# Weight loads moved from SyncE's queue to GpSimd's, unread steps left out and a new order, in an RWKV7 and SwiGLU kernel

## The chip, the cores and the metric

The kernel runs on one core of one Trainium2 chip. The metric is the device time of one execution in microseconds (us). A core has TensorE (PE; its weight loads are shown apart as PEld), VectorE (DVE), ScalarE (ACT), GpSimd (POOL) and SyncE (SP), which only issues DMAs here. POOL and ACT issue DMAs too, each in its own in-order stream.

## What is computed

The reference, cut to what matters. The shapes are B = 4, H = 8, S = 768 and D = 40; the feed-forward part has 3072 tokens, width 320 and inner width 1536.

```python
state = zeros((B, H, D, D))
for t in range(S):
    y[:, :, t] = einsum('bhd,bhde->bhe', rt, state)
    Sa = einsum('bhde,bhe->bhd', state, at)
    state = state * wt[:, :, None, :] - einsum('bhd,bhe->bhde', Sa, bt)
    state = state + einsum('bhd,bhe->bhde', vt, kt)
x = y.transpose(0, 2, 1, 3).reshape(B * S, H * D)
rms = sqrt(mean(x * x, axis=-1, keepdims=True) + 1e-06)
xn = x / rms * rms_g
g = xn @ w_gate
out = (g / (1 + exp(-g)) * (xn @ w_val)) @ w_out
```

The last state is returned to nobody: only y goes on. The feed-forward weights come in as 8-byte floats, and the kernel turns them into 4-byte floats itself.

## The kernel before

The sequence is cut into 24 chunks of 32 steps. Each chunk goes through three stages, which the code names front, inverse and main.

**front(c)** loads w, a, k, b and v of the chunk (tiles wan, kbn, wn, VU; from SP and ACT's queues for chunk 0, from POOL's for all later ones), turns them by transposes on PE, and forms by a ladder of levels 1, 2, 4, 8, 16 the products of decays. At each level it updates K (on the page `K<-K,T`; the copied half on ACT), the left factors A (at level 16 the tile aP, called Aend16 below) and the decay products T (T[32] at the end, called T32). The level's products give LT, a triangular matrix for each head and batch. LT goes out to a DRAM scratch sB and comes back, laid out otherwise, as M (8 DMAs on SP). At the end K, decayed over the whole chunk, is transposed into KN[32].

**inverse(c)** solves the triangular system on DVE in the tile Yi: 15 pairs of tensor_tensor for the first five chunks, 31 steps for later ones. The result goes out to the scratch sY and comes back into LT (8 more DMAs on SP).

**main(c)** multiplies with the state (aP times ST), solves with LT, updates the state (KN[32] times VU, the piece called update, plus the decayed old state Sdec, which uses T[32]), forms the scores and the levels, and makes y. It then takes the root mean square (a sum of squares ss, to the power -0.5 on POOL, called pow below), turns the rows and scales them by the norm's weights gcol into xg.

**feed(g)** is the feed-forward part for one or two chunks together: gate and value products on PE, SiLU on ACT, the product hT on DVE, the output product po on PE, and the result to DRAM by SP.

**narrow** turns the raw weights into 4-byte floats. The 1536 inner columns are 12 slices of 128; a slice has two halves, and 2f + h is called unit 0 to 23 in this document. An even unit has two raw loads, an odd one four, 72 in all. The raw data is laid into a tile that is not yet in use: unit u uses one of four, so it waits until unit u - 4 has been converted. Then come seven operations, with two integer tensor_scalar and three scalar_tensor_tensor operations of 480 elements among DVE's, and two on ACT.

None of these pieces is issued in the order of the code. Each call of `plan.add` makes a piece; a list ORDER names for each step which of the pieces comes next (a count from the first one not yet issued), and PAIRS says which of three PSUM pairs each room gets. So the instruction order of every engine is written out: an engine takes its pieces in this order, and a piece that waits holds back all that follow it on its engine or queue. The before kernel has 6003 pieces. Line 486 is the helper of DVE's operations, 509, 513 and 516 those of ACT's, 519 POOL's tensor_tensor, 522 and 525 its copies and memsets, 529 the helper of every DMA, 532 matmuls and 535 transposes. The raw loads are at lines 1026 to 1029, the norm's loads at 596, the ladder's end at 779 to 811 and the update at 881 to 888.

Of the kernel before, what the change touches and what calls it, by code (L numbers as in the profile page):

```python
# [16 lines left out]
P = 128  # L17
# [388 lines left out]
def kernel(  # L406
# [187 lines left out]
    for p0, kt, src in ((0, 0, 0), (0, 1, P), (0, 2, 2 * P), (64, 2, 2 * P)):  # L594
        m = min(P, DM - src)
        dma(gcol[p0:p0 + m, kt:kt + 1], moe_rms_g[src:src + m].rearrange("(d o) -> d o", o=1), "g")
# [105 lines left out]
    def kn(z, l, i, n, o):  # L702
        return z["KN"][l][half(i), kn_at(l, n, o)]
# [396 lines left out]
```

## Time and profile before

| What | Value |
|---|---|
| median of three runs | 1037.38 us (1035.87 to 1040.97) |
| the profiled execution: its time, its span | 1039.87 us, 1038.0 us |
| busy PE, DVE, ACT, POOL | 934.5, 790.2, 498.4, 306.6 us |
| share of PE in the chain that ended last | 70% |
| SyncE's queue (q1, with 42.37 MB), POOL's (q0, 22.64 MB) | 18.4%, 11.8% of 16 engines |
| one raw load on SP: 256, 224, 96, 64 KB | 4.4 to 5.5, 3.5, 3.9, 4.1 to 4.2 us to landing (medians) |
| one load on POOL: 40 KB, 80 KB | 2.6 to 2.9, 2.8 to 3.2 us to landing (medians) |

The span runs from the first to the last instruction. Busy time counts an engine's work and not its issue of DMAs, but for POOL, whose DMA instructions are work of its own and are counted. The page cuts the span into 40 slices of 26 us and gives the busy tenths of each; the granted clock of PE is shown beside them, in tenths of full speed. It is

```
PEclk 9957667899999999999999999999999999999999
```

so PE has its full clock only at the very start and from about 187 us on. In SP's view an instruction is the issue of a DMA, shown as SPq with its time; data lands later.

### The profile page before, as it was taken

The page shows a single profiled execution, that of the slowest core. Times are in us where ns is not written, and L with a number is a line of the kernel's source. Part 1 is how long each engine was busy: PE and PEld are TensorE (multiplying, and loading weights), DVE is VectorE, ACT ScalarE, POOL GpSimd, SP SyncE. Part 2 cuts the span into 40 slices and gives each one's busy share as a digit, 9 for nine tenths or more (in the row PEclk, how much of TensorE's full clock was granted, in tenths as well). Part 3 has the DMA queues.
Part 4 walks back from the last instruction along what each step waited for, and adds up shares of the span by engine and source line. Part 5 has one row for each costly group of instructions (what it writes and reads, how often), then busy time and mean ns, then how long its engine had stood idle before and what let it go on. Part 6 is the DMA issues. An engine that isn't in the chain of part 4 may idle for free.

```text
span 1038.0 us, 55525 instructions
## 1 busy us (share of the span) xinstructions
PE 934.5 (90%) x24592; PEld 760.3 (73%) x24592; DVE 790.2 (76%) x2747; ACT 498.4 (48%) x1113; POOL 306.6 (30%) x530
## 2 busy tenths in 40 slices
PE   2546767999999999999999999999999999999998
PEld 2445756877777878777778777777787787788777
DVE  8989978867869778868778679678697787777531
ACT  5566556453454464464454544534534635436131
POOL 9523234221432242233331324123232413400000
PEclk9957667899999999999999999999999999999999
DMA  7675443222242242232231232232322422420100
GB/s 159 145 173 120 99 93 82 56 63 54 43 84 38 47 95 43 60 79 42 59 84 28 62 75 55 55 68 36 76 45 55 81 41 65 75 44 8 43 7 21
DMA packets 147056, 68.89 MB, mean 66 GB/s; under 512 B 121088, under 2 KB 136384, under 8 KB 146816
## 3 DMA queue, kind: packets, MB, share of 16 engines
q1 hardware_dynamic: 128448, 42.37, 18.4%
q0 software_dynamic: 16192, 22.64, 11.8%
q8 instruction: 193, 3.16, 1.3%
q10 hardware_dynamic: 2176, 0.33, 0.2%
q14 instruction: 47, 0.39, 0.1%
HBM read 55.05 MB, written 10.22 MB: 63 GB/s over the span
## 4 chain that ended last, share of the span: by engine, by line
PE 70%; DVE 9%; DMA 7%; SPq 4%; issue 4%; ACT 2%; DVEq 0%; ACTq 0%
PE ps L532 50%; PE po L532 14%; PE ps L535 6%; SPq L529 4%; DVE Yi L486 2%; DMA LT<-sY 2%; DMA sY<-Yi 2%; DVE tmp L486 1%; DMA sB<-LT 1%; DVE LT L486 1%; DVE wf L486 1%; DMA M<-sB 1%; DVE K L486 1%; DVE y L486 1%; DVE As L486 0%
## 5 line engine op out<-in xcount | busy, mean ns | idle before, releaser
L532 PE MATMUL ps<-xg,wf 128*128 128x256 f32 (+3 forms) x1872 | 361.1, 375 | 1.1 <-DVE hT L486 0.9
L532 PEld LDWEIGHTS ps<-xg,wf 128*128 128x128 f32 (+1 forms) x1872 | 267.7, 190 | 49.1 <-issue 13.2
L532 PE MATMUL po<-wf,hT 128*128 128x320 f32 x576 | 179.7, 446 | 1.1 <-issue 1.1
L486 DVE TENSOR_TENSOR hT<-ps,sg 128x256 f32<-128x256 f32 (+1 forms) x156 | 59.8, 398 | 94.1 <-PE ps L532 56.0
L532 PEld LDWEIGHTS po<-wf,hT 128*128 128x128 f32 x576 | 102.9, 189 | 38.6 <-issue 4.0
L486 DVE TENSOR_TENSOR tmp<-Yi,M 128x24 f32<-128x24 f32 (+21 forms) x512 | 106.6, 208 | 17.4 <-DMA M<-sB 4.5
L486 DVE TENSOR_TENSOR Yi<-Yi,tmp 128x24 f32<-128x24 f32 (+21 forms) x512 | 106.8, 209 | 10.6
L509 ACT ACTIVATE sg<-ps 128x256 f32<-128x256 f32 (+1 forms) x156 | 54.0, 369 | 109.8 <-PE ps L532 106.8
L529 POOL DMA_DIRECT2D VU<-in_v_dram x92 | 53.9, 587 | 155.4 <-PE ps L532 134.4
L486 DVE TENSOR_TENSOR K<-K,T 128x512 f32<-128x512 f32 (+1 forms) x192 | 93.2, 501 | 4.4 <-PE ps L532 1.9
L519 POOL TENSOR_TENSOR ss<-ss,mhalf 128x1 f32<-128x1 f32 x24 | 14.3, 596 | 255.1 <-DVE ss L486 255.0
L532 PE MATMUL ps<-Ab,K 64*60 64x56 f32 (+2 forms) x4608 | 76.3, 220 | 12.7 <-issue 2.4
L532 PEld LDWEIGHTS ps<-Ab,K 64*60 64x60 f32 (+2 forms) x4608 | 69.3, 132 | 22.4 <-issue 10.1
L513 ACT COPY KN<-ps 128x640 f32<-128x640 f32 x96 | 65.8, 692 | 38.8 <-DVE LT L486 24.4
L529 POOL DMA_DIRECT2D kbn<-in_k_dram x92 | 54.1, 589 | 98.5 <-PE ps L532 98.5
L486 DVE TENSOR_TENSOR As<-ps,msi 128x256 f32<-128x256 f32 (+1 forms) x168 | 70.9, 453 | 15.5 <-PE ps L532 10.9
L529 POOL DMA_DIRECT2D kbn<-in_b_dram x92 | 54.1, 589 | 82.9 <-PE ps L532 81.3
L532 PEld LDWEIGHTS ps<-As,KN 128*40 128x40 f32 x3072 | 67.3, 128 | 11.6 <-issue 4.1
L532 PE MATMUL ps<-As,KN 128*40 128x32 f32 x3072 | 72.6, 208 | 2.4 <-DVE As L486 1.2
L513 ACT COPY K<-K 128x512 f32<-128x512 f32 x96 | 61.0, 636 | 27.1 <-PE ps L532 11.8
L486 DVE SCALAR_TENSOR_TENSOR Yi<-M,Yi 128x31 f32<-128x31 f32 (+6 forms) x228 | 44.5, 243 | 36.7 <-DMA M<-sB 20.0
L529 POOL DMA_DIRECT2D wn<-in_w_dram x92 | 51.8, 565 | 43.7 <-DVE KN L486 43.5
(131 smaller groups left out, 1503.4 us busy)
## 6 DMA issues: line engine op xcount, KB each, us to landing
M<-sB SPq DMA_DIRECT2D x96, 128.0 KB, 3.0
wan<-in_r_dram SPq DMA_DIRECT2D x24, 160.0 KB, 4.0
kbn<-in_k_dram POOLq DMA_DIRECT2D x92, 40.0 KB, 2.6
kbn<-in_b_dram POOLq DMA_DIRECT2D x92, 40.0 KB, 2.9
VU<-in_v_dram POOLq DMA_DIRECT2D x92, 40.0 KB, 2.7
wan<-in_w_dram POOLq DMA_DIRECT2D x46, 80.0 KB, 3.2
wan<-in_a_dram POOLq DMA_DIRECT2D x46, 80.0 KB, 2.8
wn<-in_w_dram POOLq DMA_DIRECT2D x92, 40.0 KB, 2.8
```

The source lines that it names most:

```text
L486: plan.add("DVE", time + more + each * size(o), 0.087, lambda at: [fn(at(o), *m(at))], [o], aps(*args))
L509: scalar(o, [a], lambda at: nc.scalar.activation(at(o), at(a), f, **kw), aps(acc), 0.1 if f in (AF.Square, AF.Relu) else 0.0)
L513: scalar(o, [a], lambda at: nc.scalar.copy(at(o), at(a)), extra=more)
L519: plan.add("POOL", 0.5, 0.06, lambda at: nc.gpsimd.tensor_tensor(o, a, b, op), [o], [a, b])
L529: plan.add(by, 0.6 if by == "POOL" else 0.45, 0.0, lambda at: queue.dma_start(out=o, in_=i), [o], [i], load=load, since=since)
L532: return o, lhsT, rhs, lambda at: nc.tensor.matmul(at(o), lhsT, rhs, start=start, stop=stop, skip_group_check=True), 4
L535: return o, i, ident, lambda at: nc.tensor.transpose(at(o), i, ident), 2
```

## The change

There are four parts. The raw loads of units 4 to 23 (slices 2 to 11, 60 DMAs) and the four loads of the norm's weights are issued by POOL in place of SP. Steps whose result nobody reads are left out: for chunk 0 the left factors and decays for a state that does not exist yet (aP and T[32]), for chunk 23 the last K and its copy, T[32], KN[32], Sdec and the update of the state. PAIRS is shorter by the two rooms. ORDER is a new list of 5993 pieces. The computed output is the same.

```diff
-        dma(gcol[p0:p0 + m, kt:kt + 1], moe_rms_g[src:src + m]..., "g")
+        dma(gcol[p0:p0 + m, kt:kt + 1], moe_rms_g[src:src + m]..., "g", "POOL")
...
-            K1 = K_.next()
+            if G > 1 or c + 1 < NCH:
+                K1 = K_.next()
...
+            if l == 16 and c == 0:
+                K = K1
+                break
...
-            tt(Tl[2 * l], t[:, :, :, 0], t[:, :, :, 1], MUL)
+            if G > 1 or c + 1 < NCH:
+                tt(Tl[2 * l], t[:, :, :, 0], t[:, :, :, 1], MUL)
...
-        z["KN"][32] = KN_[32].next()
+        if c + 1 < NCH:
+            z["KN"][32] = KN_[32].next()
...
-        if c > 0:
+        if 0 < c < NCH - 1:
             tt(Sdec, ST.rearrange("p n i d -> p (n i) d")[:, :, 0:D], z["T"][32].to_broadcast((P, NI, D)), MUL)
...
-        up = plan.room()
-        pe("update", [mm(up[part(o), i, col(slot(n))], kn(z, 32, i, n, o), VU[half(i), n, o, 0:D]) for n, i, o in each])
+        if c + 1 < NCH:
+            up = plan.room()
+            pe("update", [mm(up[part(o), i, col(slot(n))], kn(z, 32, i, n, o), VU[half(i), n, o, 0:D]) for n, i, o in each])
...
-                else src.bitcast(I32).rearrange("p (f w) -> p f w", w=2), load, since=S0 + S1 * f)
+                else src.bitcast(I32).rearrange("p (f w) -> p f w", w=2), load, "SP" if f < 2 else "POOL", since=S0 + S1 * f)
```

Decoded, the two lists differ as follows around the loads. SP's list before has weights between the DMAs of the first inverses (inverse 1: three sY, four raw loads, a sY, a norm load, an LT, a norm load, three LT); after, the sB, M, sY and LT groups of the first four chunks stand whole, but for the chunk's own r loads and the first M group inside inverse 0's sY. POOL's list after has the 60 raw loads among the loads of the next chunks, the memsets of the start and the pow steps: the first at place 46 of POOL's pieces, unit 13's last three right behind the first VU load of front 2, unit 21's last three behind chunk 1's pow, unit 22's second behind a kbn load of front 5, and unit 23's last three behind chunk 2's pow. DVE's and PE's lists keep the order of the stages; on DVE unit 23 is converted ahead of the first feed's third hT, where before its last three operations came after eight of them.

More of the change, by code (lines that the diff above doesn't have):

```diff
@@ L33 @@
 ORDER = """
[202 rows of a table removed]
[200 rows of a table added]
 """
 PAIRS = """
-01201210121021200021102212200010110200100201020112101002120121012212012212110202010010102012120120012002120020000011
-21210200101022100112022211110111102001222121111021211202221200012011120122122211112120211212100022010102200020101002
-20021101010001010211121111020000111210200010012212120021012112221201202122010201200001101212210212102121021020112110
-12111102101020202122221201022110100022221210101022022002020221211202011101001210222111101200200021222021210111211010
-122221012001120211200102020212021
+01201210010210202012021221120102002012011102100012202011220021012221220001021002101020200111220010221101211112220020
+10110002021210102121022002120211100120101010210201211112201202020220212020012221020202110101022011121211111212011002
+00210201011001020121010110202022122122102201111101020011112000120120122212221011010001212020021112120122220210212211
+12211212002100202200101012210010100111221210000211021201121112111222000202002010212111102110100021211012120220000221
+2102101222020212210001010212012
 """
@@ L595 @@
         m = min(P, DM - src)
-        dma(gcol[p0:p0 + m, kt:kt + 1], moe_rms_g[src:src + m].rearrange("(d o) -> d o", o=1), "g")
+        dma(gcol[p0:p0 + m, kt:kt + 1], moe_rms_g[src:src + m].rearrange("(d o) -> d o", o=1), "g", "POOL")
     blank(eye, 0.0)
@@ L778, in front @@
             t = Tl[l].rearrange("p n (g x) -> p n g x", x=2)
-            K1 = K_.next()
-            if G == 1:
-                tt(K1[:, :, :, 0:16], K[:, :, :, 0:16], t[:, :, None, :, 1].to_broadcast((P, NI, 2, 16)), MUL)
-            else:
-                for x in range(2):
-                    tt(side(K1[:, :, x], l, 0), side(K[:, :, x], l, 0), t[:, :, :, 1, None].to_broadcast((P, NI, G, l)), MUL)
-            kn_ = lambda k: k.rearrange("p n x (g h l) -> p (n x) g h l", h=2, l=l)[:, :, :, 1]
-            copy(kn_(K1), kn_(K))
+            if G > 1 or c + 1 < NCH:
+                K1 = K_.next()
+                if G == 1:
+                    tt(K1[:, :, :, 0:16], K[:, :, :, 0:16], t[:, :, None, :, 1].to_broadcast((P, NI, 2, 16)), MUL)
+                else:
+                    for x in range(2):
+                        tt(side(K1[:, :, x], l, 0), side(K[:, :, x], l, 0), t[:, :, :, 1, None].to_broadcast((P, NI, G, l)), MUL)
+                kn_ = lambda k: k.rearrange("p n x (g h l) -> p (n x) g h l", h=2, l=l)[:, :, :, 1]
+                copy(kn_(K1), kn_(K))
+            if l == 16 and c == 0:
+                K = K1
+                break
             if l == 16:
@@ L807, in front @@
             dma(M[m * BH:(m + 1) * BH].rearrange("p b x -> p (b x)")[:, 0:C * C], sB, "M")
-        z["KN"][32] = KN_[32].next()
-        copy(z["KN"][32].rearrange("p (n o e) -> p n o e", n=N, o=2),
-             turned(K.rearrange("p (n i) x s -> p n (i x s)", i=2), ins=TOP, outs=P)[:, :, :, 0:D])
+        if c + 1 < NCH:
+            z["KN"][32] = KN_[32].next()
+            copy(z["KN"][32].rearrange("p (n o e) -> p n o e", n=N, o=2),
+                 turned(K.rearrange("p (n i) x s -> p n (i x s)", i=2), ins=TOP, outs=P)[:, :, :, 0:D])
         z["aP"] = A
@@ L880, in main @@
                              U[other(i, 4 * q), :, 0:4 * D].rearrange("p o (n d) -> p o n d", n=4), more=0.09)
-        up = plan.room()
-        pe("update", [mm(up[part(o), i, col(slot(n))], kn(z, 32, i, n, o), VU[half(i), n, o, 0:D]) for n, i, o in each])
-        if c == 0:
-            copy(ST_.next()[:, :, :, 0:D].rearrange("p n i d -> p i n d"), up[:, :, 0:N * D].rearrange("p i (n d) -> p i n d", n=N))
-        elif c + 1 < NCH:
-            tt(ST_.next()[:, :, :, 0:D].rearrange("p n i d -> p i n d"),
-               up[:, :, 0:N * D].rearrange("p i (n d) -> p i n d", n=N),
-               Sdec.rearrange("p (n i) d -> p i n d", n=N), ADD)
+        if c + 1 < NCH:
+            up = plan.room()
+            pe("update", [mm(up[part(o), i, col(slot(n))], kn(z, 32, i, n, o), VU[half(i), n, o, 0:D]) for n, i, o in each])
+            if c == 0:
+                copy(ST_.next()[:, :, :, 0:D].rearrange("p n i d -> p i n d"), up[:, :, 0:N * D].rearrange("p i (n d) -> p i n d", n=N))
+            else:
+                tt(ST_.next()[:, :, :, 0:D].rearrange("p n i d -> p i n d"),
+                   up[:, :, 0:N * D].rearrange("p i (n d) -> p i n d", n=N),
+                   Sdec.rearrange("p (n i) d -> p i n d", n=N), ADD)
         if c % 2 == 0:
```

402 rows, old and new, of the table ORDER are left out of this document.

## The prediction

> **What bounds the kernel now.** I read the slices first, then the table by stretches, then who waited for whom, and last the queue of SyncE in order of time. The slices, and the stretches (columns: time, length, busy us and instructions of PE, weight loads, DVE, ACT, POOL, granted clock, DMA share, GB/s):
>
> ```profile
> PE   2546767999999999999999999999999999999998
> DVE  8989978867869778868778679678697787777531
> POOL 9523234221432242233331324123232413400000
> ...
> 0.00:25.00 25.00, 6.15 (x160) 5.45 (x160) 22.18 (x60) 13.31 (x23) 23.71 (x48) 1.00 0.73 162
> 50.00:75.00 25.00, 10.77 (x391) 9.47 (x391) 21.87 (x70) 17.47 (x30) 7.84 (x14) 0.50 0.73 168
> 125.00:150.00 25.00, 15.11 (x652) 13.21 (x654) 19.01 (x55) 14.72 (x31) 11.29 (x19) 0.70 0.50 107
> 0.00:175.00 175.00, 101.23 (x3724) 90.58 (x3728) 155.54 (x458) 102.27 (x203) 77.78 (x140) 0.74 0.55 126
> 187.00:1033.00 846.00, 822.68 (x20478) 660.13 (x20478) 627.63 (x2271) 386.22 (x891) 225.68 (x385) 1.00 0.27 54
> ```
>
> There are two stages. Up to about 175 us DVE is the bound: it is busy for 155.5 of 175 us, mostly with the weights' conversion and the chunks, and PE waits for what it makes. From 187 us PE is busy for 822.7 of 846 us and sets the pace. So the end moves by what the first stage gains or loses, plus PE work that goes from the second. The raw weights all load in the first stage.
>
> Where does DVE lose its 175 - 155.5 = 19.5 us there? Its waits between 55 and 100 us, then between 100 and 176 us:
>
> ```profile
> DVE tmp L486 <- ACT Yi L513: 2.2, 1, 2.2
> DVE exs L486 <- ACT exs L509: 1.2, 1, 1.2
> DVE K L486 <- PE ps L532: 0.8, 1, 0.8
> DVE exs L486 <- DMA wf<-in_moe_w_gate_dram: 0.8, 1, 0.8
> ```
> ```profile
> DVE tmp L486 <- DMA M<-sB: 4.5, 2, 3.7
> ```
>
> The first group (exact gaps 2.17 + 1.24 + 0.78 + 0.75 = 4.9 us) has SyncE's queue behind or beside it. The queue itself, at the end of the second inverse:
>
> ```profile
> 75.24 3.13 SPq L529 DMA_DIRECT2D sY<-Yi  x3
> 78.41 0.60 SPq L529 DMA_DIRECT2D wf<-in_moe_w_out_dram  x1
> 79.05 0.98 SPq L529 DMA_DIRECT2D wf<-in_moe_w_val_dram  x2
> 80.08 0.59 SPq L529 DMA_DIRECT2D wf<-in_moe_w_gate_dram  x1
> 80.72 0.60 SPq L529 DMA_DIRECT2D sY<-Yi  x1
> 81.36 1.44 SPq L529 DMA_DIRECT2D gcol<-in_moe_rms_g_dram  x1
> 84.89 0.33 SPq L529 DMA_DIRECT2D LT<-sY  x1
> 85.26 1.59 SPq L529 DMA_DIRECT2D gcol<-in_moe_rms_g_dram  x1
> 86.90 1.58 SPq L529 DMA_DIRECT2D LT<-sY  x3
> ```
>
> Four weight loads stand ahead of the last sY and a norm load inside the LT group: from the last Yi (75.2) to the last LT landing (90.4) 15.2 us pass. Inverse 0 needs 15.4 (50.1 to 65.5); inverse 10, with no weights about, 7.9. So each of the first two inverses hands its result on some 7 us late.
>
> **The change part by part.** The words of both ORDER lists decode into pieces, in number 6003 and 5993, and the trace shows each engine's instructions in the order of the first list, so each piece of before has its time and sums can be made along the second list.
>
> *Dropped steps.* DVE loses 5 pieces, ACT 3, PE 2. In front 0, Aend16 (0.41 us) and T32 (0.17; 0.1 net of the overlap with its neighbour) leave DVE while it is the bound: **-0.5**. Of the last chunk, the K1, T32 and Sdec steps (0.68, 0.17, 0.82 us on DVE at 958 to 961) and two ACT copies (0.62, 0.70) lie under a full PE: 0. The transposes of K are PE work there: 0.67 us at 969.45, overlapping the next group, **-0.6** at most; I take it. The last chunk's update is the last PE piece of all:
>
> ```profile
> 1032.90 0.83 PE L532 MATMUL ps<-VU,KN 64*40 64x40 f32 x64
> 1033.01 0.43 ACT L513 COPY o<-po 128x320 f32<-128x320 f32 x1 [1.71 <-PE po L532]
> 1033.46 1.98 SPq L529 DMA_DIRECT2D out_dram<-o  x4
> ```
>
> It runs beside the copy and the output DMAs, which do not wait for it: 0.
>
> *SyncE's queue.* 60 raw loads leave it (34.3 us of issue) and 4 norm loads (4.0 us). In the new list sY and LT of inverses 0 to 3 stand without a weight between them. What DVE gets is not the 7 us twice, since it worked on weights meanwhile, but its waits: **-4.9** for the first group, if nothing takes their place. Bounds: 0, and all waits after the first 30 us, 13.9. The wait for M<-sB (3.7 at 145.8) has no weight ahead of it (sB 134.8, M 139.7 to 141.9, Yi 145.8); I leave it.
>
> *POOL's queue.* 64 DMAs come. POOL's own rows are 0.56 to 0.65 us each (kbn 0.582), so 64 x 0.58 = 37 us beside the 77.8 busy of 175: it fits on average. Order is the risk, since an instruction waiting on POOL holds all behind it. I added up the busy time of each engine along the new list (DVE plus some 3.5 us for waits that stay) and 4 us for a landing (the wf loads' median runs from 3.5 to 5.5). Unit 4 (a unit is half a slice): last raw issued at 32.6, landed 36.6, DVE there at 36.9. Unit 5: 48.3 against 48.5. Unit 9 stands behind a wn load that waits for front 1's KN product (about 56): landed 62.3, needed 62.6. Unit 13 stands behind the first VU load of front 2, which waited for PE until 73.96; with inverse 0 handed on some 5 us earlier it goes at 69, and its data lands at 75.5, needed at 78. The last units come behind POOL's pow of chunks 1 and 2, which waits for DVE's ss, and behind a kbn load that waits for chunk 2's level products. For unit 23: pow, raw, wn, two raws take 3.3 us after ss and land 4 us later, 7.3, while DVE has 4.9 us of work in between: it waits 2.4. Unit 22 likewise some 1.2, unit 21 none. DVE has already begun to wait for PE there (0.84 at 175.9, 2.64 at 182.0), so of these 3.6 I count **+1.5**; bounds 0 and 8.
>
> *POOL's DMAs beside DVE.* A tensor_scalar of 480 takes 0.40 us. 18 of them met a POOL DMA, with mean 0.44 and worst 0.75 (11.18). With 35 us of raw issue spread over 140 us, about 17 of the 40 to come meet one: 17 x 0.035 = **+0.6**; bounds 0 and 40 x 0.35 = 14. [...]
>
> *The new order.* In PE's list each chunk's solve stands within two places of where it was (150 for 149, 565 for 566, 1029 for 1029). PE's waits listed from 190 to 1033 us sum to 22.5 us, so an order could give or cost some 5 either way; I take 0.
>
> **Sum**: -0.5 - 0.6 - 4.9 + 1.5 + 0.6 = -3.9. The profiled execution took 1039.87 (span 1038.0, with 1.9 around it) and would take 1036.0; it lies 2.5 above the median of the runs, 1037.38, from which I forecast **1033.5**.
>
> **Rivals.** (B) The two early inverses pull everything ahead: the 8.2 us of DVE waits between 100 and 176 us (4.5, 1.5, 0.8, 0.8, 0.5 and small ones) go too: 1033.5 - 8.2 = 1025.3. For it: chunk 0's and 1's results come 5 to 7 us sooner, and POOL sits idle for PE 33 us in that stage. Against: M<-sB follows DVE's own LT, not the queue. (C) POOL's order takes over, slower: if unit 13's loads wait for VU until 74 (2.5 us late) and units 21, 22 and 23 cost 1, 3 and 4, DVE loses 10.5 and the first group of waits merely changes its name: 1037.4 - 1.1 + 0.6 + 10.5 = 1047.4. It decides as soon as raw data lands after DVE's sum; the margins above are 0 to 2.5 us. (D) Nothing but the dropped work: DVE and PE fill the time anyway, 1037.4 - 1.1 = 1036.3. (E) GpSimd's DMAs and DVE shut each other out: at the worst row, 14 in place of 0.6: 1046.9. [...]
>
> **How the numbers follow.** Forecast 0.40, B 0.30, C 0.14, D 0.13, E 0.03. About 0.5% (5.2 us: below 1032.2, above 1042.6) is what a measurement here can tell from no change. Of the forecast's case, whose own range is 1030 to 1037, 0.07 falls below 1032.2. Faster 0.30 + 0.07 = 0.37; same 0.33 + 0.13 = 0.46; slower 0.17. The range reaches to B with a little beyond and halfway into C: 1024 to 1044.
>
> **What would show it.** Right: sY and LT of inverses 0 and 1 without a break, some 8 to 10 us from the last Yi to the last LT; the 2.2 us wait for Yi at 60 gone; PE full from about 183; tail as before. Wrong: DVE waits on exs or o behind wf or exs DMAs, above all at units 9, 13, 22 and 23 (C); tensor_scalars of 480 well above 0.45 us in the mean (E); PE waits after 190 us far from 22.5 us, which would put the difference into the order.

## The result and the profile after

The changed kernel is slower: median 1045.74 us of 16 runs (1037.6 to 1055.28), beside 1037.04 us (1030.49 to 1042.12) for 16 runs of before on the same chip; the ratio is 1.0066, 95% interval 1.0041 to 1.009. The ratio is that of the fast runs: two runs of after that lie over 1.5% above its fastest, 1053.56 and 1055.28 us, are not in it. Its profiled execution took 1045.07 us with a span of 1043.3. The forecast was 1033.5, with 1024 to 1044 as its range: the time lies above its upper end, and the change of 0.7% goes the other way.

The slices of after, in the same columns as before:

```profile
PE   3456677999999989999999999899899999999998
DVE  9899978877967967868878679678587697776531
```

And two of its stretches:

```profile
0.00:175.00 175.00, 102.35 (x3900) 92.26 (x3900) 158.65 (x463) 105.30 (x206) 113.24 (x199) 0.71 0.54 125
187.00:1038.50 851.50, 820.17 (x20422) 657.40 (x20416) 624.58 (x2259) 384.25 (x888) 227.86 (x388) 1.00 0.27 54
```

In the first 175 us DVE does 3.1 us more work than before (158.65 against 155.54), with POOL's 35 us more of issue beside it. From 187 us PE is busy for 820.2 us (822.7 before), but in a stretch of 851.5 us in place of 846. The time goes there, in the stage that I had left alone. The queue of SyncE did what the change says; behind the last Yi of inverse 1 no weight stands any more:

```profile
73.25 2.80 SPq L527 DMA_DIRECT2D sY<-Yi  x4
79.22 1.81 SPq L527 DMA_DIRECT2D LT<-sY  x4
```

The last LT lands near 83 us, about 10 us after that Yi, where before took 15.2. What PE waited for from 190 us on, before (the first fence) and after (the second):

```profile
PE ps L532 <- issue: 12.2, 16, 1.8
...
PE ps L535 <- issue: 1.5, 1, 1.5
PE po L532 <- issue: 1.1, 1, 1.1
```
```profile
PE ps L530 <- issue: 14.8, 19, 1.7
PE ps L533 <- issue: 3.1, 3, 2.6
...
PE po L530 <- issue: 1.3, 1, 1.3
```

Most of it is "issue": PE waited for nothing that the profile shows as a releaser, 14.8 us before and 19.2 after. All idle gaps of PE from 190 us on sum to 31.3 us, by the same count 23.3 before. That was on my list of what would prove me wrong, and it pointed at the order.

### The profile page after: what moved, and what is told of

Its sections match the earlier page's. It is cut to its first block, busy times and chain, and to the rows that moved or that the text cites. A ratio compares the mean times of both kernels' runs of the same rounds, so it can differ in the third digit from the quotient of the medians.

```text
span 1043.3 us, 55333 instructions
## 1 busy us (share of the span) xinstructions
PE 932.7 (89%) x24512; PEld 758.5 (73%) x24512; DVE 791.1 (76%) x2742; ACT 496.4 (48%) x1110; POOL 345.6 (33%) x594
## 4 chain that ended last, share of the span: by engine, by line
PE 62%; DVE 15%; DMA 7%; issue 5%; SPq 4%; POOL 3%; ACT 3%; DVEq 0%; POOLq 0%; ACTq 0%
PE ps L530 43%; PE po L530 13%; PE ps L533 6%; SPq L527 4%; DVE Yi L484 4%; DMA M<-sB 3%; DVE tmp L484 3%; DMA sB<-LT 2%; DVE y L484 2%; DVE As L484 2%; DVE wf L484 1%; DVE LT L484 1%; DMA wf<-in_moe_w_gate_dram 1%; DMA sY<-Yi 1%; DVE exs L484 1%
## 5 line engine op out<-in xcount | busy, mean ns | idle before, releaser
L530 PE MATMUL po<-wf,hT 128*128 128x320 f32 x576 | 182.0, 450 | 2.6 <-DVE hT L484 1.3
L484 DVE TENSOR_TENSOR K<-K,T 128x256 f32<-128x256 f32 (+1 forms) x191 | 92.4, 498 | 2.1 <-PE ps L530 1.1
L530 PE MATMUL ps<-Ab,K 64*60 64x56 f32 (+2 forms) x4608 | 78.1, 223 | 17.4 <-ACT KN L511 5.6
L530 PEld LDWEIGHTS ps<-Ab,K 64*60 64x60 f32 (+2 forms) x4608 | 71.6, 136 | 27.0 <-issue 10.8
L511 ACT COPY KN<-ps 128x640 f32<-128x640 f32 x95 | 65.2, 693 | 42.3 <-DVE LT L484 31.1
L484 DVE TENSOR_TENSOR As<-ps,msi 128x256 f32<-128x256 f32 (+1 forms) x168 | 69.9, 454 | 16.0 <-ACT As L514 11.5
L517 POOL TENSOR_TENSOR ss<-ss,mhalf 128x1 f32<-128x1 f32 x24 | 15.9, 664 | 176.4 <-DVE ss L484 176.4
L511 ACT COPY K<-K 128x512 f32<-128x512 f32 x95 | 60.2, 634 | 24.0 <-DVE K L484 10.3
```

The source lines that it names most:

```text
L484: plan.add("DVE", time + more + each * size(o), 0.087, lambda at: [fn(at(o), *m(at))], [o], aps(*args))
L511: scalar(o, [a], lambda at: nc.scalar.copy(at(o), at(a)), extra=more)
L517: plan.add("POOL", 0.5, 0.06, lambda at: nc.gpsimd.tensor_tensor(o, a, b, op), [o], [a, b])
L530: return o, lhsT, rhs, lambda at: nc.tensor.matmul(at(o), lhsT, rhs, start=start, stop=stop, skip_group_check=True), 4
```

## The experiments

Pieces are counted along an order; all times below are of profiled executions, all ratios are to before on the same chip. A list that has one order in front and the other behind holds the same pieces. "The new order" means ORDER together with its PAIRS: the PAIRS of after are not only shorter by two rooms but another assignment (311 of the 495 entries differ from those of before without the two rooms), every kernel below with another ORDER has its own PAIRS, and no run tells the two apart. The expectations call the last hT of the first feed "the last hT of unit 0"; in the text it is feed 0, the last of the 13 is feed 12.

**e1 and e2: which part of the order.**

```diff
-ORDER = the new list                   (e1; loads on POOL as in after)
+ORDER = the new list to its 1417th piece (231 us), the old one behind
...
-ORDER = the new list                   (e2)
+ORDER = the old list to its 1417th piece, the new one behind
-                ..., load, "SP" if f < 2 else "POOL", since=S0 + S1 * f)
+                ..., load, "SP", since=S0 + S1 * f)
-        ..., "g", "POOL")
+        ..., "g")
```

> The changed kernel, with the new order for its first 1417 pieces (up to about 231 us) and the old order for all that follow. Theory O (the new order of the later stage, where PE is the bound, loses some 9 us, and the start with its loads on POOL gains 3.6): about 1033.5, a ratio of 0.996 to before, last hT of the first feed near 211.5 us as in the changed kernel, PE gaps after 190 us near 23 us as before. Rival Q (what loses is the move of the loads to POOL, by something that lasts): about 1045, ratio 1.007. Rival S (any new joint of orders costs): slower than before, with the loss right after 231 us.

> All raw and norm loads on SP, the old order for the first 1417 pieces and the new order for the rest, steps dropped. Theory O: no gain at the start, all of the loss later: 1037 + 9 = 1046, ratio 1.008, PE gaps after 190 us near 31 us. Rival Q: 1036 to 1037, ratio 0.999, gaps near 23 us.

e1: 0.9992 (0.9966 to 1.0019). e2: 1.0089 (1.0061 to 1.0117). The loss goes with the new order behind piece 1417, whichever queue the weights are on. The gain of the start that e1 was to show (0.996) is not there in its time. In e2 PE's idle gaps from 190 us on sum to 25.8 us and not to 31; more of its loss is time at half clock (17.1 us, below). Their late stages, e1 first:

```profile
187.00:1024.00 837.00, 815.21 (x20330) 652.86 (x20326) 620.12 (x2249) 384.66 (x889) 226.93 (x388) 1.00 0.26 55
```
```profile
187.00:1037.00 850.00, 823.99 (x20324) 660.75 (x20323) 625.04 (x2256) 384.06 (x889) 226.07 (x385) 0.99 0.25 54
```

The same number of matmuls within six takes PE 815.2 us in e1 and 824.0 in e2, where the granted clock is 0.99 in the mean.

**e3 and e4: is the queue move apart from the order?** e3 is after with the old list throughout; e4 is after with the loads back on SP (the diff of e2 without its ORDER).

> The changed kernel with the old order throughout (less the dropped pieces), so the moved loads stand on POOL where they stood on SP in the common list. Theory O: the later stage as before (gaps near 23 us); the start between a gain of 4 (the inverses go out unhindered) and a loss of 8 (loads behind waiting POOL instructions), as the order was not made for it: 1033 to 1045. Rival Q: about 1045 with the gaps after 190 us near 31 us.

> The changed kernel with its new order, but all raw and norm loads on SP. Theory O: the loss of the later stage stays (gaps near 31 us) and the gain of the start goes or turns to a loss: 1046 to 1054, ratio 1.009 to 1.016. Rival Q: back at 1037, gaps near 23 us.

e3: 1.0088 (1.0057 to 1.012). e4: 1.0254 (1.0224 to 1.0284). e4 lost more than either theory said. Both lose in the start: the last hT of feed 0 comes at 223.5 and 228.6 us (after: 211.3). On the other queue than the one it was made for, an order left DVE waiting. In e4, DVE's waits from 30 to 180 us:

```profile
DVE tmp L484 <- DMA M<-sB: 8.1, 2, 6.8
DVE exs L484 <- ACT exs L507: 4.9, 3, 4.1
DVE exs L484 <- DMA wf<-in_moe_w_gate_dram: 4.8, 2, 4.6
```

The stage behind feed 0 takes e3 813.3 us, as in the kernels with the old order (table below). So the queue move has no lasting cost of its own, and it was not free to make without a new start order.

**e5: the dropped steps alone.** The new code with the old list less the dropped pieces and all loads on SP.

> The unread steps dropped and nothing else: the order of before, every raw load on SyncE. Theory D (the shorter start seen with the new start and with the old one alike comes from the dropped steps): the last hT of unit 0 near 211 us, where before has 215.1, ratio near 0.996. Theory M (it comes from the queue move): the last hT of unit 0 near 214.5 us, ratio 0.9995. By either, the stage after unit 0 lasts what it lasted in before (816 us to the last hT of unit 12, within 3).

1.0014 (0.9991 to 1.0036): nothing measurable. The last hT of feed 0 came at 209.9 us, which is theory D's number, but e18, the same kernel, has 213.7: one profile does not tell the theories apart.

**What "issue" is.** PE's list of after has 49,277 instructions. After 187 us it has 39 spacings over 0.55 us between two weight loads (those behind an output matmul of 320 columns left out, where 70 of 100 are 0.63 us). Of these, 19 stand at places that leave 192 or 193 when divided by 256; no other remainder occurs twice. In before it is 15 of 31, at the same two remainders. The trace has a queue that fits this (columns: packets, MB, share):

```profile
q8 instruction: 192, 3.15, 1.3%
```

192 packets of 16,384 bytes: one for each 256 instructions of PE. Before has 193 of them for 49,457 instructions. So its instructions come in blocks; the place between two blocks is called a border here. In after, where PE waited at a border, the packet of the next block started 0.9 us (median) after PE had entered the block before it, took 0.9 to 1.3 us, and PE went on 1.4 us (median) after its end, some 3.3 us in all. Of the blocks that PE ran in under 2.3 us, 9 of 12 ended in a wait of over 0.3 us (mean 1.64); between 2.3 and 3.1 us, 10 of 19 (mean 0.70); between 3.1 and 3.6 us, 4 of 11; over 3.6 us, 1 of 118. The quick blocks are those of short matmuls. The longest of these waits (columns: start, us, engine, line, operation, count, idle before):

```profile
372.81 0.78 PE L530 MATMUL ps<-ST,aP 64*32 64x40 f32 x64
373.52 0.79 PE L530 MATMUL ps<-VU,LT 32*32 32x40 f32 x64
374.25 0.38 PE L533 MATMUL ps<-ident,wan 64*104 64x64 f32 x6
377.18 0.49 PE L533 MATMUL ps<-ident,wan 64*104 64x64 f32 x10 [2.56 <-issue]
```

The transposes of chunk 8's r stop after the sixth of sixteen. The block that ends there was run in 1.56 us; the packet of the next one started at 374.67 and took 0.92. The new order has 64 + 64 + 16 short matmuls in a row here, 288 instructions. In before the same transposes follow four long matmuls and take 0.66 us, not 3.42:

```profile
365.60 1.34 PE L532 MATMUL po<-wf,hT 128*128 128x320 f32 x4
366.88 0.66 PE L535 MATMUL ps<-ident,wan 64*104 64x64 f32 x16
```

A replay follows from that: take the starts of PE's instructions from one trace, take the border waits out, set a border every 256 instructions from another first place, and let each block last at least 3.1 us. It gives 16.3 us for before (the trace has 19.1 after 187 us) and 22.2 for after (24.2). Instructions added early move every border behind them:

```diff
-    plan.warm = lambda: nc.tensor.matmul(po_[:, 0, DM:DM + P], ident, ident, start=False, stop=False, ...)
+    plan.warm = lambda: nc.tensor.matmul(po_[:64, 0, DM:DM + 56], ident[:64, :64], ident[:64, :56], start=False, stop=False, ...)
...
+    18 (e6), 56 (e7) or 64 (e8) words "-" in ORDER behind the first PE piece: so many calls of plan.warm, four instructions each
```

> The kernel after with 72 more TensorE instructions (18 small matmuls into an unread strip of PSUM, two passes of a load and a matmul each) right after its first piece, where TensorE is idle from 8 to 14.5 us; nothing else. Theory F (TensorE's instructions arrive in blocks of 256; a block that is run in less than about 3.1 us makes it wait for the next, and the new order puts more such quick blocks in a row of pieces): the block borders move by 72 instructions, and the trace of after, replayed with borders there, has 16.6 us of such waits after 187 us in place of 22.2: 5 to 6 us faster than after, ratio to before 1.001 (0.998 to 1.003). Theory W (the new order loses by the waits of its pieces for each other, not by where the blocks end): no change, ratio 1.0066.

> The kernel after with 224 more TensorE instructions (56 small matmuls) at the same place; nothing else. Theory F: the replay with borders there has 31.0 us of waits in place of 22.2, so 9 us slower than after, ratio to before 1.015 (1.011 to 1.019). Theory W: no change, ratio 1.0066.

> The kernel after with 256 more TensorE instructions (64 small matmuls) at the same place: one whole block, so the borders fall between the same pieces as in after. Control. Theory F and theory W: no change, ratio 1.0066 (1.004 to 1.009). If the added matmuls themselves cost something, it shows here.

e6: 1.0048 (1.0022 to 1.0073), above F's range and not clear of W's 1.0066. e7: 1.0172 (1.0139 to 1.0204). e8, the control: 1.0171 (1.0143 to 1.02), far from the 1.0066 expected: the added matmuls took 109 ns each and held up the start by 6 us. So the times of e7 and e8 tell nothing about borders. Their traces do: border waits of 15.9, 31.1 and 24.5 us, where the replay of after said 16.6, 31.0 and 22.2. In e9 and e10 the added matmuls write afresh (start=True, stop=True), 18 and 64 of them; e11 is e5 with 54.

> As e6, but the 18 added matmuls write afresh in place of adding up, which should take under 1 us of TensorE's idle time in place of 4. Theory F: 16 to 17 us of waits at block borders after 187 us, where after has 24.9 by the same count; 5 to 8 us faster than e10 beside it on this chip, ratio 0.999 to 1.002. Theory W: no difference from e10.

> Control, as e8 with the short matmuls: 256 more instructions, so the block borders fall where they fall in after. The added matmuls of e8 took 109 ns each, 13.9 us in all, and held up the start (last hT of unit 0 at 217.2 us, where after has 211.3); here some 4 us of idle time. Theory F and theory W: the ratio of after, 1.0066, and 24 to 25 us of waits at block borders. If it stays at 1.017, the added matmuls cost in another way and e7 is not to be read.

> The drop-only kernel of e5 (the order of before, every load on SyncE) with 216 more TensorE instructions (54 short matmuls) in TensorE's first idle stretch. Theory F: the replay of e5 has 25.5 us of border waits there in place of 17.5: the old order loses 8 us by where its blocks end alone, ratio 1.0014 + 0.0077 = 1.009 (1.005 to 1.013). Theory W: no change from e5, ratio 1.0014.

e9: 1.0078 (1.005 to 1.0107); e10: 1.0124 (1.0083 to 1.0164); they still took 109 ns each, so e10 is no clean control. e9's median is 3.7 us below e10's, but the last hT of feed 0 comes 3.6 us earlier in it (211.4 against 215.0), and 1.0078 is no better than after: on times, theory F is not shown in the new order. e11: 1.0076 (1.0049 to 1.0103), with 23.4 us of border waits; the last hT of feed 0 comes at 212.9 us (e5 209.9, e18 213.7). The old order is 6 to 8 us slower with the same pieces in the same order, of which its start explains 3 at most: where the blocks end costs time by itself, as F said and W did not. Part of that comes by the clock: e11's stage has 6.8 us at half clock, e5's none and e18's 3.4. The transposes at 376 us in e9:

```profile
376.13 0.48 PE L530 MATMUL ps<-VU,LT 32*32 32x40 f32 x30 [0.90 <-issue]
376.55 0.66 PE L533 MATMUL ps<-ident,wan 64*104 64x64 f32 x16
```

and in e10, whose borders fall as in after:

```profile
377.16 0.38 PE L534 MATMUL ps<-ident,wan 64*104 64x64 f32 x6
380.31 0.77 PE L534 MATMUL ps<-ident,wan 64*104 64x64 f32 x10 [2.77 <-issue]
```

In e9 the border has moved into the piece ahead and costs 0.90. In all twenty profiles this piece takes 3.1 to 4.5 us where the new order meets the old borders (after, e2, e4, e8, e10, e14, e17) and 0.65 to 0.66 in the others.

**e12 to e15: where in the order, and a better mix.** By the times at which both orders have done the same pieces (but for a few), the new one was 2.4 us shorter from 234 to 352 us and lost 9 us from 352 to 680.

```diff
-ORDER = the new list
+ORDER = e12: new to the 2127th piece (352 us), old behind
+ORDER = e13: new, but old from the 2127th to the 4074th piece (680 us)
+ORDER = e14: e1, but new from the 2127th to the 4074th piece
+ORDER = e15: e12 with 18 words "-" as in e9
```

> The kernel after with the new order up to its 2127th piece (about 352 us) and the old one from there, loads on GpSimd as in after: e1 with a later seam. The stretch from 234 to 352 us was 2.4 us shorter in the new order, the rest 9 us longer. A replay made of the trace of after up to the seam and of e1 behind it has 13.1 us of border waits, e1 17.3. Theory F: 2 to 6 us faster than e1 and e5, ratio 0.995 to 0.998. Theory W: 2 us faster than e1, ratio 0.997 to 0.999. It may be the fastest of all.

> The kernel after, with the old order only from its 2127th to its 4074th piece (352 to 680 us), the new one before and behind, loads on GpSimd. Theory F+W (the loss sits in this stretch, half of it waits at block borders, half waits of pieces for each other with the slow clock behind them): a replay made of the traces of after and of e1 loses 8 us of border waits (14.2 in place of 22.2) and 4.8 us of other waits: 12 us faster than after, ratio 0.995 (0.992 to 0.999). Theory N (the loss is spread over the whole new order, or comes from the start): 2 to 4 us faster than after, ratio 1.003 to 1.005.

> The reverse: e1 with the new order only from the 2127th to the 4074th piece. Theory F+W: the replay gains 6.9 us of border waits (24.2 in place of 17.3) and 4.8 us of other waits: ratio to before 0.9992 + 0.011 = 1.010 (1.005 to 1.014). Theory N: 1 to 3 us slower than e1, ratio 1.000 to 1.003.

> e12 (the new order to the 2127th piece, the old one behind) with 72 more TensorE instructions in TensorE's idle time, as in e9. Theory F: the replay of e12 has 14.7 us of border waits there in place of 17.2: 1 to 3 us faster than e12, ratio 0.990 (0.987 to 0.993). Theory W: as e12, 0.992.

e12: 0.992 (0.989 to 0.995), below both theories' ranges, though its border waits were 16.1 us where the replay said 13.1. e13: 0.9982 (0.9959 to 1.0005). e14: 1.006 (1.0032 to 1.0088). e15: 0.9973 (0.9947 to 1.0). e13 and e14 fall into F+W's ranges at their weak ends and outside N's: the stretch from 352 to 680 us carries most of the loss in both directions. In the traces PE's instructions of this stretch take 323.0 to 326.1 us in four kernels with the new order there (after, e2, e14, e17) and 312.8 to 314.6 in four with the old one (e1, e5, e12, e13). e13's border waits fell less than the replay said (about 18 us, not 14.2). e15 missed: the replay said 14.7 us of border waits, its trace has 18.3, so the fixed 3.1 us is good for a sum to some 4 us and no better.

> e12 once more, beside the drop-only kernel and after on one chip. If e12's gain is the kernel's and not that run's: ratio 0.992 (0.989 to 0.996), border waits 15 to 18 us after 187 us, no stretch at half clock before the tail.

> The kernel after once more, the control for e6 to e10, which ran without it: ratio 1.0066 (1.003 to 1.010), border waits 23 to 26 us, the piece that turns r of the eighth chunk again 3.4 to 4.5 us long.

> The drop-only kernel once more, beside e16: ratio 1.0014 (0.998 to 1.004), border waits 17 to 19 us. The queue move with the new order to unit 2, by itself, is e16 against this: 0.991 if e12 and e5 hold.

On one chip: e16 0.995 (0.9922 to 0.9978), e17 1.0061 (1.003 to 1.0092), e18 0.9995 (0.9968 to 1.0022). So e12's kernel, the change with the old order behind 352 us, is faster than before by some 0.5 to 0.8%, and than after by some 1.1% (e16 against e17). But e16's border waits are 18.2 us and it has two stretches at half clock, against 16.1 and none in e12: its expectation on these missed, and one profile can lie 8 us from another of the same kernel.

The sums by kernel (us; the stage is from the last hT of feed 0 to the last of feed 12; "other" are PE's gaps away from borders; half clock is the time in the stage at a granted clock of 0.5; another way to count a border wait moves single entries by up to 2.5 us):

| kernel, order behind feed 0 | feed 0 | stage | border waits | other | half clock |
|---|---|---|---|---|---|
| before; e5; e18; e1; e3: old | 215.1; 209.9; 213.7; 209.1; 223.5 | 816.3; 810.9; 812.3; 813.1; 813.3 | 19.1; 16.9; 17.3; 17.4; 18.4 | 7.4; 5.8; 5.4; 7.0; 4.6 | 0; 0; 3.4; 0; 3.4 |
| after; e17; e2; e4: new | 211.3; 214.3; 211.1; 228.6 | 826.2; 822.0; 824.4; 820.7 | 24.2; 21.8; 21.5; 23.8 | 11.1; 8.8; 7.8; 5.7 | 6.8; 6.8; 17.1; 6.8 |
| e6; e9: new, borders by 72 | 211.4; 211.4 | 818.1; 822.5 | 15.9; 16.8 | 10.1; 11.5 | 10.2; 13.7 |
| e7: new, by 224 | 210.8 | 829.5 | 31.1 | 6.1 | 10.2 |
| e11: old, by 216 | 212.9 | 818.9 | 23.4 | 4.3 | 6.8 |
| e12; e16: mixed | 207.2; 208.9 | 806.5; 814.9 | 16.1; 18.2 | 2.8; 5.1 | 0; 6.8 |

Means of the first two rows: the stage 813.2 and 823.3, **+10.1**. Border waits 17.8 and 22.8, **+5.0**. Other gaps 6.0 and 8.4, **+2.3**. Half clock 1.4 and 9.4, of which half is counted as lost, an estimate from the granted 0.50: **+4.0**. The three make 11.3, a little over the loss. The half clock follows gaps. In after it comes at 676.1 and 754.6 us; three stretches around the first, with the granted clock in the column ahead of the DMA share:

```profile
672.70:676.10 3.40, 1.00 (x37) 0.79 (x38) 3.30 (x12) 0.94 (x3) 0.00 (x0) 1.00 0.03 5
676.10:679.50 3.40, 3.40 (x70) 3.16 (x72) 3.30 (x13) 0.00 (x0) 0.00 (x0) 0.50 0.00 0
679.50:683.00 3.50, 3.50 (x89) 2.95 (x88) 2.29 (x12) 1.01 (x3) 0.58 (x1) 1.00 0.07 16
```

PE was idle for 2.4 of 3.4 us, waiting for ACT's y and DVE's As; for the next 3.4 us it runs at half speed.

Not settled: e6 and e9 have the border waits of the old order and still a stage of 820.3 us in the mean, 7 over it, with more of the other gaps and of half clock. So by the sums some half of the loss stands at borders and the rest is waits of the new order's pieces for each other and the slow clock behind gaps; but moving the borders in the new order made the stage only 3.0 us shorter in the mean, with no gain in time that is clear of the noise, and no run here takes only the other waits away. What the new PAIRS have to do with these is open too.

## Why the prediction was wrong

**The step that failed** is "The new order ... PE's waits listed from 190 to 1033 us sum to 22.5 us, so an order could give or cost some 5 either way; I take 0." It cost 10.1 us in the stage; with the -2.4 below, 1037.0 - 2.4 + 10.1 = 1044.7, near the measured 1045.74. Two errors stand in it. I compared where each chunk's solve stands in PE's list and found it within two places, but in the costliest place it was what stands directly behind what: 128 short matmuls ahead of 16 short transposes, which then took 3.1 to 4.5 us in place of 0.66. And I took the sum of waits as a bound, with no look at what they are: 14.8 of them were "issue", which no releaser explains, and which rose to 19.2 with the new order. The slow clock behind a gap was no term at all.

**The queue, -4.9**: inverse 1 is handed on after some 10 us in place of 15.2 and the wait for Yi at 60 us is gone, as forecast. But the time did not come from there. DVE's waits from 30 to 100 us are 2.9 to 4.1 us in the seven profiles with the new start on POOL and nothing added (after, e1, e12, e13, e14, e16, e17), and 5.3, 2.3, 1.9 and 3.4 in the four with the old start on SP (before, e2, e5, e18): the 4.9 us were mostly peculiar to the one profile of before, and others took their place. From 100 to 176 us they are 4.7 to 6.9 us against 8.6 to 10.3, so what was gained lies where rival B looked for it, in part and with the new order of the start beside it. The last hT of feed 0 has a mean of 210.1 us in the seven and 212.4 in the four. That is -2.4, dropped steps included, with 5 to 7 us between profiles of like starts, so it is not clear of the spread.

**POOL's order, +1.5**, and rival C: in after DVE waits 3.7 us for wf data and for ACT's exs between 30 and 100 us, and not at all for raw data from 100 to 176 us, where the 1.5 was looked for. C's 10.5 us do not appear. In e3, whose order was not made for it, DVE waits 5.3 us for wf data and feed 0 ends 10 to 14 us later than in e18 and e5. **POOL's DMAs beside DVE, +0.6**, and rival E: the 480-element tensor_scalars have a mean of 421 ns in after and 443 in before, where two took 0.80 and 1.23 us beside a MEMSET of POOL; the 33 of after that met a POOL DMA have 428, the others 404. Nothing of 14 us. POOL's raw issues in after have means of 0.57 to 0.65 us, and the longest took 0.80. That the two shut each other out, as E had it, no run shows.

**Dropped steps, -1.1**: e5 and e18 say 1.0014 and 0.9995, no gain that can be told from none. **The tail, 0**: as forecast, 5.5 us from the last hT to the end in after and 6.3 in before.

The chance of 0.17 for slower stood on C and E; what came was slower by another way, one that was not among the rivals.

## What to carry to other kernels

Where an engine is busy for 97% of a stage, an order of its instructions is no neutral part of a change: list its waits with "issue" apart from those with a releaser, and see at which places of the instruction list they fall. Runs of very short instructions may be better spread between long ones, so that each block of 256 lasts longer than its successor takes to come (3.1 to 3.6 us here); that follows from the counts above, and no run tried it by itself. A new order can be tested in parts by joining it to the old one; e12 kept the part that gained and left the part that lost.

## What the runs showed of the hardware

- PE's instructions came in packets of 16,384 bytes, one for each 256 (192 packets for the 49,277 instructions of after, 193 for the 49,457 of before), and PE mostly waited where a block was run in less than some 3 us (in after behind 9 of 12 blocks under 2.3 us and 1 of 118 over 3.6): 16 (e6) to 31 us (e7) of a 1030 us kernel. Where PE waited in after, the packet of the next block started 0.9 us (median) after PE had entered the block before it; the waits look like a lead of no more than one block.
- The stretches at half clock in the stage behind feed 0 last 3.4 us or twice that and start on one grid of 3.413 us in each trace (in after at 676.09 and 754.60 us, 23 steps apart). In the step of that grid ahead of them PE was idle for 1.2 to 2.9 us (in after 2.4 and 1.4); the most idle step that had none behind it had 1.8 (in after 1.5). So half clock came at times behind 1.2 us of idleness in pieces, and not always behind 1.8.
- 128 matmuls of 64x64 by 64x56 into one place took 13.9 us, 109 ns each, whether they added up (e8) or wrote afresh (e10); 64 of like shape, each with its own operands and place, took 1.97 us in the same first 25 us (after, e6), 31 ns each. Why was not tried.
- Of the nine 480-element tensor_scalars that took over 1.0 us in the twenty profiles, eight (1.02 to 2.00 us) ran beside a MEMSET of POOL (in before 1.23 us at 75.12). Others met a MEMSET and took 0.40 to 0.85. Why was not tried.
- Kernels with the same first 1417 pieces and the same loads reach the last hT of feed 0, which lies in that part, between 207.2 (e12) and 214.3 us (e17). What sets this was not found.
